# A long convolution and a feed-forward on one core: one pass over 2048 tokens rewritten as two halves of 1024, with a written-out instruction order

## The chip, the cores and the metric

The kernel runs on one core of one Trainium2 chip. The metric is device time in microseconds (us) of one execution; it is the median of three runs. The engines are PE (TensorE: matmuls; "PEld" are its weight loads), ACT (ScalarE), DVE (VectorE), POOL (GpSimd) and SP (SyncE, which issues the DMAs). Matmuls write to PSUM, eight banks of 512 float32 per partition, and ACT or DVE copy ("evict") the results to SBUF.

## The reference

```python
def layernorm(x): return (x - mean(x)) / sqrt(var(x) + 1e-5)      # over the last axis

def A(q, k, v, shift_k, ssm_k, ssm_D):         # [1, 2048, 640]
    k_shift = causal_conv(k, shift_k)          # 4 taps
    kv = k_shift * v
    y = causal_conv(kv, ssm_k)                 # 2048 taps per channel, by rfft/irfft of length 4096
    return q * (y + kv * ssm_D)

def B(x, w1, b1, w2):                          # 640 -> 1728 -> 640
    h = x @ w1 + b1
    return (h * tanh(softplus(h))) @ w2        # Mish

x = A_q
h = x + A(layernorm(x), A_k, A_v, A_shift_k, A_ssm_k, A_ssm_D)
out = h + B(layernorm(h), B_w1, B_b1, B_w2)
```

All tensors are bfloat16. `B_x` is not used. The long convolution is computed by matmuls with trigonometric tables: transform the filter, transform the signal, multiply, transform back.

## The kernel before

Tokens are numbered t = 16·p + t2, with p on the 128 partitions, so a "tile" t2 is one of 16 sets of 128 tokens. The 640 channels come in five blocks `dc` of 128. The stages are:

- **Filter**: `k1pe` (line 560) transposes the filter on PE. `s1k` (lines 510 and 511) is the first transform step: pairs of matmuls with 64 output rows each. `s2k` (line 539) is the second step: 128 matmuls per group of channels against the table G. Five DMAs load the filter rows. G (128x128x128) is built on DVE by `gb` (line 483) from a table R of 1 MB.
- **Signal**: `kspe` (line 586) does the four-tap shift by matmuls on k, which is loaded by a transposing DMA (line 476). `kv` (line 597) multiplies by v on DVE. `s1v` and `s2v` use the same lines 510, 511 and 539.
- **Product**: `swap` (line 639) copies the spectrum with its upper and lower 64 partitions exchanged, by DMA. `prod` (line 720) multiplies on DVE.
- **Back**: `i1pe` (lines 731 and 732), then per tile `i2pe` (line 782).
- **Per tile, after `i2pe`**: `lnx` (line 789, ACT, the first layernorm applied), `wb` (793) and `h` (797) on DVE, `ln2` (802, 803, 419) on DVE, the power -0.5 on POOL (422), `dr` (812, DVE, the second layernorm applied), five PE transposes (819) and an eviction into the transposed activations `lnhT`.
- **Feed-forward**: in units of 128, 128, 256, 512, 512 and 512 tokens (`UNITS`). Per unit come 14 blocks of 128 hidden rows (the last is half zeros), five matmuls each (845) and a Mish on ACT (851). Per tile come 28 matmuls of 320 columns (861), a residual add on DVE (870) and a DMA out.

Every PSUM eviction is `ev`, on ACT (line 390) or on DVE (line 392). `_schedule` builds the order of all engines at build time from a planner's durations, with a priority for each operation in the table `PRIO`. The whole convolution stands before the feed-forward: `i2pe` reads all of the back transform's first step, and that reads all products. From `i1pe` on, PE is kept busy by idle matmuls (`fill`, line 830).

Of the kernel before, what the change touches and what calls it, by code (L numbers as in the profile page):

```python
# [16 lines left out]
S = 2048  # L17
D = 640
FF = 1728
P = 128  # L20
NDC = 5
NDG = 160
NFC = 14
FP = NFC * P
EPS = 1e-5
UNITS = [128, 128, 256, 512, 512, 512]
CHAIN = [80, 80.5, 81, 81.5] + [100.3, 100.31, 101.3, 101.31] + [102.3, 102.31, 102.32, 102.33] + [103.3, 103.31, 103.32, 103.33]
GRP_DC = [[0, 1], [2, 3], [4]]
GRP_DG = [(32 * g[0], 32 * g[-1] + 32) for g in GRP_DC]
NGRP = len(GRP_DC)  # L30
Q_KN = ("sp",) * NDC
Q_R = "sp"
Q_V = "sp"
Q_SWAP = "sp"
KTP = 16 + S
PRIO = {
# [34 lines left out]
}  # L71

OFF_KP = 0
OFF_KPS = 40960
OFF_KN = OFF_KPS
OFF_KT = OFF_KN + 20480
OFF_G = OFF_KT + NDC * KTP * 2
OFF_B = OFF_G + 32768
OFF_V = OFF_B + 40960
OFF_KK = OFF_V + 20480  # L80
OFF_XA = OFF_KK + 8192
OFF_KVB = OFF_XA + 8192
OFF_END = OFF_KVB + 12288
OFF_KVB2 = OFF_KK
OFF_R = OFF_XA
OFF_W1 = OFF_G
OFF_W2 = OFF_KPS
OFF_LNHT = OFF_KP
OFF_UB0 = OFF_KP + 20480
OFF_UB1 = OFF_KPS + 17920  # L90
OFF_T2M = OFF_KVB
OFF_LNX = OFF_KVB + 8192
OFF_HC = OFF_XA
OFF_OB = OFF_XA + 3840

class _Ring:


    def __init__(self, slots):
        self.slots = slots  # L100

_CELL = {}

class _RT:
    def __init__(self, ring, name=""):
        self.ring = ring
        self.name = name
        self.users = []
        self.tile = None
        self.slot = None  # L110

class _Op:
    __slots__ = ("name", "opts", "deps", "allocs", "emit", "prio", "lat", "start", "finish", "eng", "done", "picks", "cap", "xbar")

    def __init__(self, name, opts, deps, allocs, uses, emit, prio, lat):
        self.name = name
        self.opts = opts if isinstance(opts, list) else [opts]
        self.deps = deps
        self.allocs = list(allocs)
        for rt in list(allocs) + list(uses):  # L120
            rt.users.append(self)
        self.emit = emit
        self.prio = prio
        self.lat = lat
        self.start = None
        self.finish = None
        self.eng = None
        self.done = False
        self.cap = 0.0
        self.xbar = False  # L130

_WIN = 0.3
_SEM = 0.18
_OWN = {"act": 0.1, "dve": 0.1}
_FIRST = 0.6
_LAST_BYTE = 1.6

def _stage(name):
    m = re.match(r"(k1|s1k|s2k|kp|ks|kv|s1v|s2v|x|prod|i1|gb|d_swap|c_diag|d_kn|d_kT|d_R|d_v)(?:pe|ev)?(\d*)(?:_.*)?$", name)
    if not m:  # L140
        return name
    st = {"kp": "s2k", "x": "s2v"}.get(m.group(1), m.group(1))
    return st + m.group(2)

def _schedule(ops):
# [12 lines left out]
    for o in reversed(ops):  # L158
        m = 0.0
        for c in children.get(id(o), []):  # L160
            v = bl[id(c)] + o.lat
            if v > m:
                m = v
# [763 lines left out]
```

## Time and profile before

| | |
|---|---|
| runs | 241.54, 241.96, 243.04 us; median 241.96 us |
| profiled execution, span | 238.7 us from the first instruction to the last |
| granted TensorE clock | 1.000 |
| busy | PE 221.0, DVE 155.5, ACT 139.5, POOL 20.3 us |
| DMA | 25.52 MB in 20049 packets |

"Busy" is the time in which at least one instruction of the engine ran. The span is 3.3 us less than the median of the runs; that is what lies around it. A profile's group names line, engine, operation, output <- input, shapes and count; then busy time in all, the mean duration of one in ns, and idle time just before them with what ended it. Since an instruction can start before the one ahead has ended, busy time divided by count is the pace, and it is shorter than the mean duration.

The first feed-forward matmul starts at 101.53 us and the last one's residual add at 234.91 us.

### The profile page before, as it was taken

To read this page: it belongs to the slowest core of one execution; us is meant where nothing else is said; L and a number is where in the kernel's file an instruction comes from. 1 tells how busy PE (TensorE), PEld (TensorE's weight loads), DVE (VectorE), ACT (ScalarE), POOL (GpSimd) and SP (SyncE) were. 2 spreads that over 40 slices of the span, in tenths; PEclk is the share of its full clock that TensorE was granted. 3 is DMA by queue.
4 is the path that set the end of the run, shared out by engine and by line. 5 is a ranking of instruction groups with operands and counts; after the bars stand their busy time and mean duration, and the time that the engine had idled before them with its cause. 6 is when DMAs were issued, how large, how long until landed. Compare 5 with 4: busy or idle time off the path is not lost.

```text
span 238.7 us, 7414 instructions
## 1 busy us (share of the span) xinstructions
PE 221.0 (93%) x3266; PEld 167.2 (70%) x3266; DVE 155.5 (65%) x318; ACT 139.5 (58%) x192; POOL 20.3 (9%) x39
## 2 busy tenths in 40 slices
PE   8888688988779999999999999999999999999993
PEld 3777577888779998698788764577744677545772
DVE  0998967899979998899999898584350332100121
ACT  2668676989998999589166456930156401366000
POOL 2500000000000003022311200210000000000000
PEclk9999999999999999999999999999999999999999
DMA  6999999806999797000000000001000001000001
GB/s 235 393 340 228 173 181 225 124 3 150 238 233 388 236 368 292 5 3 3 27 30 1 27 30 0 0 4 55 27 30 0 0 30 52 31 0 3 27 27 55
DMA packets 20049, 25.52 MB, mean 107 GB/s; under 512 B 11633, under 2 KB 15538, under 8 KB 19634
## 3 DMA queue, kind: packets, MB, share of 16 engines
q1 hardware_dynamic: 19760, 24.88, 37.5%
q8 instruction: 25, 0.41, 0.7%
q10 hardware_dynamic: 146, 0.18, 0.5%
q0 software_dynamic: 112, 0.01, 0.1%
q14 instruction: 6, 0.05, 0.1%
HBM read 14.57 MB, written 2.62 MB: 72 GB/s over the span
## 4 chain that ended last, share of the span: by engine, by line
PE 77%; ACT 10%; issue 4%; DVE 4%; DMA 3%; SPq 0%; ACTq 0%; DVEq 0%
PE banks L861 26%; PE banks L845 25%; ACT arena L390 9%; PE banks L539 6%; PE banks L731 4%; PE banks L732 4%; PE banks L782 3%; DMA arena<-tab_R 3%; PE banks L510 3%; PE banks L586 2%; DVE arena L392 2%; PE banks L819 2%; PE banks L560 1%; PE banks L830 1%; PE banks L511 1%
## 5 line engine op out<-in xcount | busy, mean ns | idle before, releaser
L390 ACT CAST arena<-banks 128x1024 bf16<-128x1024 f32 x78 | 73.2, 1046 | 16.3 <-PE banks L511 10.6
L845 PE MATMUL banks<-arena 128*128 128x512 bf16 (+2 forms) x420 | 62.3, 308 | 0.3 <-ACT arena L390 0.2
L861 PE MATMUL banks<-arena 128*128 128x320 bf16 x448 | 62.0, 299 | 0.2 <-DVE arena L793 0.2
L851 ACT ACTIVATE arena<-banks,b1s 128x512 bf16<-128x512 f32 (+2 forms) x84 | 43.5, 546 | 27.6 <-PE banks L845 25.5
L861 PEld LDWEIGHTS <-arena 128*128 128x128 bf16 x448 | 43.6, 98 | 17.1 <-issue 0.4
L845 PEld LDWEIGHTS <-arena 128*128 128x128 bf16 x420 | 35.3, 98 | 25.7 <-issue 0.7
L870 DVE TENSOR_TENSOR arena<-banks,arena 128x640 bf16<-128x640 f32 x16 | 13.2, 824 | 43.3 <-PE banks L861 43.2
L539 PE MATMUL banks<-arena 128*128 128x64 bf16 (+1 forms) x768 | 25.3, 188 | 4.6 <-ACT arena L390 2.9
L392 DVE CAST arena<-banks 128x1024 bf16<-128x1024 f32 x22 | 26.3, 1221 | 4.5 <-PE banks L511 2.2
L390 ACT COPY arena<-banks 128x640 bf16<-128x640 bf16 (+1 forms) x12 | 8.6, 746 | 32.7 <-PE banks L819 32.5
L539 PEld LDWEIGHTS <-arena 128*128 128x128 bf16 x768 | 23.3, 97 | 6.2 <-issue 5.1
L720 DVE TENSOR_TENSOR arena<-arena 128x1024 bf16<-128x1024 bf16 x40 | 24.8, 687 | 2.2 <-ACT arena L390 1.7
L510 PE MATMUL banks<-consts,arena 128*64 128x128 bf16 x320 | 21.3, 220 | 3.4 <-ACT arena L390 2.0
L511 PE MATMUL banks<-consts,arena 128*64 128x128 bf16 x320 | 21.6, 221 | 0.0
L511 PEld LDWEIGHTS <-arena 128*64 128x64 bf16 x320 | 18.4, 110 | 3.4 <-issue 3.2
L731 PE MATMUL banks<-consts,arena 128*128 128x128 bf16 x160 | 18.8, 219 | 1.3 <-DVE arena L392 0.9
L510 PEld LDWEIGHTS <-arena 128*64 128x64 bf16 x320 | 18.7, 110 | 1.7 <-issue 1.0
L732 PE MATMUL banks<-consts,arena 128*128 128x128 bf16 x160 | 18.7, 219 | 0.0
L732 PEld LDWEIGHTS <-arena 128*128 128x128 bf16 x160 | 15.6, 98 | 1.3 <-issue 1.0
L731 PEld LDWEIGHTS <-arena 128*128 128x128 bf16 x160 | 15.6, 98 | 0.6 <-issue 0.6
L789 ACT ACTIVATE arena<-arena,nmr_75,r1v 128x640 bf16<-128x640 bf16 x16 | 14.4, 926 | 2.6 <-DVE nmr_75 L684 1.4
L392 DVE COPY arena<-banks 128x1024 bf16<-128x1024 bf16 (+1 forms) x14 | 8.0, 598 | 11.8 <-PE banks L819 11.7
(47 smaller groups left out, 181.0 us busy)
## 6 DMA issues: line engine op xcount, KB each, us to landing
arena<-arena SPq DMA_DIRECT2D x20, 256.0 KB, 6.0
arena<-in_A_ssm_k_dram SPq DMA_DIRECT2D x5, 512.0 KB, 8.2
arena<-in_A_v_dram SPq DMA_DIRECT2D x2, 1280.0 KB, 15.4
arena<-in_A_q_dram SPq DMA_DIRECT2D x8, 320.0 KB, 5.6
out_dram<-arena SPq DMA_DIRECT2D x16, 160.0 KB, 1.8
arena<-in_B_w_dram SPq DMA_DIRECT2D x5, 432.0 KB, 8.4
arena<-in_B_w_dram SPq DMA_DIRECT2D x6, 320.0 KB, 4.8
arena<-tab_R SPq DMA_DIRECT2D x1, 1024.0 KB, 7.4
```

Source lines behind the costliest of these rows:

```text
L390: clock.append(nc.scalar.copy(o, i))
L392: nc.vector.tensor_copy(o, i)
L510: nc.tensor.matmul(ps1[0:64, gl, :], lhs, fcfs_b[:, 0, :], start=True, stop=True)
L511: nc.tensor.matmul(ps1[64:128, gl, :], lhs, fcfs_b[:, 1, :], start=True, stop=True)
L539: nc.tensor.matmul(ps2[:, c0:c0 + nd], G_t()[:, f0 + fl, :], src[:, f0 + fl, :], start=True, stop=True)
L720: nc.vector.tensor_tensor(kp, x, kp, ALU.mult)
L731: nc.tensor.matmul(pz[:, gl, :], KP_t()[:, dg, :], a12_b[:, 0, :], start=True, stop=False)
L732: nc.tensor.matmul(pz[:, gl, :], KPS_t()[:, dg, :], a12_b[:, 1, :], start=False, stop=True)
L789: nc.scalar.activation(lnx.tile, xn_t()[:, t2, :], ACT.Identity, scale=r1v[:, t2:t2 + 1], bias=nmr1[:, t2:t2 + 1])
L845: nc.tensor.matmul(ph[:, 0:w], w1_t()[:, dc, fc * P:(fc + 1) * P], lnhT_t()[:, dc, c0:c0 + w], start=(dc == 0), stop=(dc == NDC - 1))
L851: nc.scalar.activation(ub_t[u % 2]()[:, fc, 0:w], rt.tile[:, 0:w], ACT.Mish, bias=b1s[:, fc:fc + 1], scale=1.0)
L861: nc.tensor.matmul(po[:, hf2 * 512:hf2 * 512 + 320], hb[:, fc, tl * P:(tl + 1) * P], w2_t()[:, fc, hf2 * 320:(hf2 + 1) * 320], start=(fc = ...
```

## The change

The kernel is written anew. The arithmetic is the same up to the way that the convolution is cut.

- **Two halves.** Tokens 0 to 1023 (h = 0) and 1024 to 2047 (h = 1) each have eight tiles, t = 8·p + t2 inside the half. With filter halves h0, h1 and signal halves x0, x1, the first output half is h0*x0 and the second h0*x1 + h1*x0, at transform length 2048. So four spectra are made (`h0`, `x0`, `h1`, `x1`), each with 10 first-step operations `s1pe` and 11 second-step operations `s2pe` (of 12 frequencies, the last of 8; matmuls of 80 columns). The spectrum of x1 also takes in kvb0 through a second table (`facc`).
- **Products.** Half 0 has 22 (`p1`, `p2`). Half 1 has 22 of h1 with x0 (`p1b`, `p2b`), 22 of x1 with h0 (`p1x`, `p2x`) and 22 additions (`paX0`, `paP2`), all of 960 elements a partition (the last of 640), on DVE.
- **Swaps.** 12 DMAs for half 0, and 44 chunked ones for half 1 into three slots `kps`; the spectrum chunk of half 1 has two slots `kpc`.
- **Loads.** R is 0.5 MB; k, v, x and the filter are loaded half by half, those of half 1 partly block by block into two slots each.
- **Per tile.** The chain `lnx`, `i2pe`, `wb`, `h`, `ln2`, `ln2s`, `dr` stays. The addition of epsilon moves from DVE to POOL. The five PE transposes and their eviction give way to one transposing DMA from SBUF to SBUF (`d_tr`), issued by SP.
- **Feed-forward.** Units of 256 tokens, six of them, and a last one of 512. The 14th block, of 64 hidden rows, is no longer padded: its two token halves go to the two 64-column halves of PE. The last tile is cut in 512 and 128 columns.
- **Order.** `_schedule` and `PRIO` go. `ORDER` lists all operations with engine and PSUM slot; each engine runs its own in that sequence. The feed-forward of half 0 (`m1pe0` to `m1pe3`, `m2pe0` to `m2pe7`) stands among the transforms of half 1. There are no fill matmuls.

The core of the difference:

```diff
-UNITS = [128, 128, 256, 512, 512, 512]
+HS = 1024
+NDG = 80
+NT = 8
+CH = [(f, min(12, P - f)) for f in range(0, P, 12)]
+UNITS = [(0, 2), (2, 2), (4, 2), (6, 2), (8, 2), (10, 2), (12, 4)]
...
+                for gl in range(8):
+                    lhs = src()[:, gi * 8 + gl, :]
+                    for ri in range(2):
+                        v.nc.tensor.matmul(pz[64 * ri:64 * ri + 64, gl, :], lhs, v.fcfs[:, ri, :], start=True, stop=acc is None)
+                    if acc is not None:
+                        lha = v.buf(acc, [P, NDC, 16, 64])[:, dc, gi * 8 + gl, :]
+                        for ri in range(2):
+                            v.nc.tensor.matmul(pz[64 * ri:64 * ri + 64, gl, :], lha, v.facc[:, ri, :], start=False, stop=True)
...
-                nc.tensor.transpose(pt[:, dc * P:(dc + 1) * P], hc.tile[:, dc * P:(dc + 1) * P], ident_b)
+        dma(f"d_tr{T}", 164e3, lambda e: v.nc.sync.dma_start_transpose(lnT(T), hc()), r=[("row", sl)], w=[lnT_key(T)], kind="dmax")
...
+                    if fc < 13:
+                        v.nc.tensor.matmul(ph[:, 0:w], w1[:, dc, fc * P:(fc + 1) * P], rhs(dc, 0, w), start=(dc == 0), stop=(dc == NDC - 1))
+                    else:
+                        for q in range(2):
+                            v.nc.tensor.matmul(ph[64 * q:64 * q + 64, 0:w // 2], w1[:, dc, FL:FF], rhs(dc, q * w // 2, (q + 1) * w // 2), start=(dc == 0), stop=(dc == NDC - 1))
...
+        kps = swap_chunk("x1", n, ci, "KP0")
+        rt = s2("x1", ci, "Bx1")
+        s2ev("x1", ci, rt, lambda ci=ci: kc(ci), [("kpc", ci % 2)])
+        kp = ("kpc", ci % 2)
+        g.op(f"p2x_{ci}", "dve", lambda e, n=n, ci=ci: v.nc.vector.tensor_tensor(ks(n, ci), kc(ci), ks(n, ci), ALU.mult), r=[kp], w=[kps], kind="tt2", arg=nf * NDG)
...
+            g.op(f"pa{acc}_{ci}", "dve", lambda e, acc=acc, src=src, f0=f0, nf=nf: v.nc.vector.tensor_tensor(
+                spec(acc)[:, f0:f0 + nf, :], spec(acc)[:, f0:f0 + nf, :], src(), ALU.add), r=[key], w=[(acc, ci)], kind="tt2", arg=nf * NDG)
...
-    order = _schedule(ops)
...
+ORDER = """
+    consts:act small:pool d_kn0_1:sp warmset:dve d_kn0_0:sp pewarm:pe:0 tab:act d_R:sp d_kn0_2:sp d_b1:pool d_kn0_4:sp d_kn0_3:sp d_kT0_2:sp d_v0:sp
...
+    i1pe1_2:pe:3 lnx9:act i1ev1_6:dve i1pe1_7:pe:1 lnx8:act ln1f_10:dve i1ev1_2:dve i1ev1_7:act lnx10:act i2pe8:pe:2 i2pe9:pe:0 wb8:dve i2pe10:pe:3
+    wb9:dve i2pe12:pe:1 h8:dve i2pe11:pe:2 ln2_8:dve i2pe13:pe:0 h9:dve ln2s_8:pool ln2_9:dve dr8:dve ln2s_9:pool wb10:dve d_tr8:sp h10:dve
+    i2pe15:pe:3 dr9:dve ln2_10:dve d_tr9:sp ln2s_10:pool lnx11:act dr10:dve d_tr10:sp wb11:dve lnx12:act h11:dve m1pe4_8:pe:0 ln2_11:dve m1pe4_10:pe:1
...
+"""
...
+    with tc.manual_schedule():
+        for name, eng, slots in _order():
+            o = ops.pop(name)
+            for x, s in zip(o.allocs, slots):
+                x["slot"] = x["ring"][s]
+            o.emit(eng)
```

More of the change, by code (lines that the diff above doesn't have):

```diff
@@ L96 @@
[L96 to L110, printed above, removed]
-class _Op:
[L113 to L130, printed above, removed]
@@ new lines, with __init__, _touch, op @@
+class _Op:
+    def __init__(self, name, opts, emit, kind, arg):
+        self.name, self.opts, self.emit, self.kind, self.arg = name, opts, emit, kind, arg
+        self.deps, self.allocs, self.uses = set(), [], []
+        self.nbytes = 0
+class _Graph:
+    def __init__(self):
+        self.ops = []
+        self.seen = {}
+    def _touch(self, op, spec, write):
+        name, *key = spec if isinstance(spec, tuple) else (spec,)
+        keys = None if not key else frozenset(key[0]) if isinstance(key[0], (set, range, list)) else frozenset((key[0],))
+        for other, past in self.seen.items():
+            if other == name:
+                for o, k, w in past:
+                    if (w or write) and (k is None or keys is None or k & keys):
+                        op.deps.add(o)
+            elif other in BUFS and name in BUFS:
+                (a, n), (b, m) = BUFS[other], BUFS[name]
+                if a < b + m and b < a + n:
+                    for o, k, w in past:
+                        if w or write:
+                            op.deps.add(o)
+        past = self.seen.setdefault(name, [])
+        if write and keys is None:
+            past.clear()
+        past.append((op, keys, write))
+    def op(self, name, opts, emit, r=(), w=(), allocs=(), uses=(), kind="", arg=0, after=()):
+        o = _Op(name, [opts] if isinstance(opts, str) else list(opts), emit, kind or name, arg)
+        for x in r:
+            self._touch(o, x, False)
+        for x in w:
+            self._touch(o, x, True)
+        o.deps |= set(after)
+        for x in uses:
+            o.deps |= set(x["ops"])
+        for x in allocs:
+            o.allocs.append(x)
+            x["ops"] = []
+        for x in list(allocs) + list(uses):
+            x["ops"].append(o)
+        o.uses = list(allocs) + list(uses)
+        o.deps.discard(o)
+        self.ops.append(o)
+        return o
@@ L296, in _make_tables @@
[L296 to L297 removed]
+    R0 = np.zeros((2, NT, 8, P, 2, 8))
+    R0[0, :, :, :, 0, :] = c[:, None]
+    R0[1, :, :, :, 0, :] = s[:, None]
+    R0[0, :, :, :, 1, :] = -s[:, None]
+    R0[1, :, :, :, 1, :] = c[:, None]
+    T["R"] = R0.reshape(P, 2048).astype(np.float32).astype(bf)
@@ new lines, in _make_tables @@
+    mask = np.zeros((2, NT, 8, 8))
+    for d in range(8):
+        mask[:, :, d, d] = 1.0
+    th = 2 * np.pi * g[:, None] * t2[None, :] / 8
+    cg, sg = np.cos(th), np.sin(th)
+    A1 = np.zeros((2, 8, 8, 2, NT, 8))
+    A2 = np.zeros((2, 8, 8, 2, NT, 8))
+    for d in range(8):
+        A1[0, d, :, 0, :, d] = cg
+        A1[1, d, :, 0, :, d] = -cg
+        A1[0, d, :, 1, :, d] = sg
+        A1[1, d, :, 1, :, d] = -sg
+        for r in range(2):
+            A2[r, d, :, 0, :, d] = -sg
+            A2[r, d, :, 1, :, d] = cg
@@ L301, with _order @@
+"""
+def _order():
+    for w in ORDER.split():
+        name, eng, *slots = w.split(":")
+        yield name, eng, [int(s) for s in slots]
 @with_exitstack
@@ L362, with buf @@
     psum = ctx.enter_context(tc.tile_pool(name="psum", bufs=1, space=PSUM))
-    arena = pool.tile([P, OFF_END // 2], BF16, name="arena")
-    def view(shape, off):
+    arena = pool.tile([P, O_END // 2], BF16, name="arena")
+    v.banks = psum.tile([P, 8 * 512], F32, name="banks")
+    def buf(name, shape):
+        off, size = BUFS[name]
         n = int(np.prod(shape[1:]))
-        v = arena[:, off // 2:off // 2 + n]
-        names = "abc"[:len(shape) - 1]
+        assert 2 * n <= size, name
+        x = arena[:, off // 2:off // 2 + n]
+        names = "abcde"[:len(shape) - 1]
@@ L485 @@
-    for h in range(2):
-        DMA(f"d_v{h}", 1.31e6, (lambda e, h=h: ENG_Q[Q_V].dma_start(v_t()[:, h * 8:(h + 1) * 8, :], vview[:, h * 8:(h + 1) * 8, :])),
-            w=[("v", h)], prio=1.3 + 0.01 * h, q=Q_V)
-    def ring(name, n):
-        return _Ring([((name, i),) for i in range(n)])
-    R_KK = ring("kk", 2)
-    R_KVB = ring("kvb", 5)
-    R_XA = ring("xa", 4)
-    def slot(ring, rt, name, shape, off, size):
-        rt.tile = view(shape, off + rt.slot[0][1] * size)
-        return rt.tile
@@ L898 @@
-    global _LAST
-    _LAST = order
+            x = x.rearrange("p (" + " ".join(names) + ") -> p " + " ".join(names), **dict(zip(names, shape[1:])))
+        return x
+    v.buf = buf
+    v.consts = small.tile([P, 944], BF16, name="consts")
+    v.ident = v.consts[:, 0:128]
+    v.fcfs = v.consts[:, 128:384].rearrange("p (a f) -> p a f", a=2)
+    v.facc = v.consts[:, 384:640].rearrange("p (a f) -> p a f", a=2)
+    v.id32 = v.consts[:, 640:672]
+    v.a12 = v.consts[:, 672:928].rearrange("p (a f) -> p a f", a=2)
@@ new lines @@
+    v.mask = v.consts[:, 928:944].bitcast(F32)
+    for name, shape, dt in (("mhalf", [P, 16], F32), ("sk_b", [P, NDC, 4], BF16), ("diagm", [P, NDC * 4, 32], BF16), ("b1b", [P, NFC], BF16),
+                            ("b1s", [P, NFC], F32), ("st1", [P, 4, 2, 6], F32), ("mv1", [P, 16, 2], F32), ("r1v", [P, 16], F32), ("nmr1", [P, 16], F32),
+                            ("mv2", [P, 16, 2], F32), ("r2", [P, 16], F32), ("dumm", [P, 8], BF16)):
+        setattr(v, name, small.tile(shape, dt, name=name))
@@ L901 @@
+    ops = {o.name: o for o in plan(v)}
+    with tc.manual_schedule():
+        for name, eng, slots in _order():
[3 more added lines that the diff above has]
+            o.emit(eng)
+    assert not ops, list(ops)
 _INS = ['A_q', 'A_k', 'A_v', 'A_shift_k', 'A_ssm_k', 'A_ssm_D', 'B_x', 'B_w1', 'B_b1', 'B_w2']
```

1172 lines of the change are left out of this document (497 added, 675 removed), and 34 rows, old and new, of the table PRIO.

## The prediction

> **What bounds the kernel now.** I read the stretches of the span first, then the groups by shape, then the chain that ended last.
>
> The busy time of each engine in stretches (columns: PE, PEld, DVE, ACT, POOL, clock, DMA share, GB/s):
>
> ```profile
> 8.00:94.30 86.30, 74.13 (x2142) 69.52 (x2137) 77.45 (x125) 74.59 (x80) 4.94 (x11) 1.00 0.91 237
> ...
> 25.00:36.00 11.00, 7.80 (x323) 7.38 (x316) 8.33 (x15) 7.33 (x8) 0.00 (x0) 1.00 1.07 181
> 36.00:56.00 20.00, 17.58 (x597) 16.23 (x593) 17.32 (x20) 17.34 (x19) 0.00 (x0) 1.00 0.58 108
> ...
> 78.00:94.30 16.30, 16.30 (x354) 15.89 (x352) 16.02 (x35) 16.03 (x18) 1.72 (x7) 1.00 0.88 312
> 101.50:238.70 137.20, 132.94 (x1015) 89.27 (x1014) 70.12 (x174) 58.91 (x105) 12.37 (x19) 1.00 0.06 20
> ```
>
> There are two kernels in one. Up to 94.30 us (filter, signal, product, back transform) ACT and DVE are the bound: both 98% busy at the end, less in 25 to 56 us, where at first DMA is full. PE's 74 us there are mostly overlap of short matmuls. From 101.5 us PE is the bound: 132.94 of 133.4 us up to the last matmul, with DVE and ACT half idle. So the way to gain is to lay the first kernel's evictions beside the second's matmuls; and what can be gained is limited by PE's own sum.
>
> The groups by shape, busy and mean:
>
> ```profile
> L390 ACT CAST arena<-banks 128x1024 bf16<-128x1024 f32 x78 | 73.2, 1046 | 16.3 <-PE banks L511 10.6 <-PE banks L539 3.7 <-DVE arena L392 0.8
> ...
> L392 DVE CAST arena<-banks 128x1024 bf16<-128x1024 f32 x22 | 26.3, 1221 | 4.5 <-PE banks L511 2.2 <-PE banks L539 1.9 <-issue 0.2
> L720 DVE TENSOR_TENSOR arena<-arena 128x1024 bf16<-128x1024 bf16 x40 | 24.8, 687 | 2.2 <-ACT arena L390 1.7 <-DMA arena<-arena 0.5
> ```
>
> Busy by count gives paces: ACT eviction of 1024 0.94 us, DVE 1.20, DVE product of 1024 0.62. In the same way from other groups: Mish 0.686 (512 wide), 0.464 (256); `lnx` 0.90; `wb` 0.82; `h` 0.49; one layernorm's statistics 1.09 (two of 0.44, one of 0.21); `dr` 0.44; `gb` 0.47; `kv` 0.62; bf16 eviction 0.625 on DVE.
>
> The chain that ended last, in order of time (start, us, what), gives PE's paces:
>
> ```profile
> 79.90 3.54 PE banks L539 x128
> ...
> 120.53 7.64 PE banks L845 x70
> ...
> 204.55 15.11 PE banks L845 x70
> 219.66 15.23 PE banks L861 x112
> 234.91 0.82 DVE arena L870
> ```
>
> A matmul of 512 columns takes 0.216 us, of 256 0.109, of 320 0.136, of 64 0.0277. From other lines of the chain: 128 columns 0.056 (L819 x5 in 0.28), a filter transpose 0.0725 (16 in 1.16), a shift matmul 0.0185 to 0.023 (64 in 1.18, 68 in 1.57; I take 0.0205). A first-step pair of 64-row matmuls starts every 0.055 us in the order of time, so the two run side by side.
>
> **The change part by part.** PE's sum after: first step 30 x 16 plus 10 x 32 matmuls at 0.0277 = 22.2; second step 44 operations, 512 matmuls of 80 columns at 0.0358 (between 0.0277 for 64 and 0.056 for 128) = 18.3; back transform 320 x 0.0556 = 17.8; shift 440 x 0.0205 = 9.0; filter transposes 80 x 0.0725 = 5.8; `i2pe` 16 x 0.55 = 8.8; warm-up 3.3; first feed-forward product 58.8 (six units of 65 x 0.109 + 5 x 0.056, one of 65 x 0.216 + 5 x 0.109); second 448 x 0.136 = 60.9. Together 205. The same sum before is 209 plus 4 of fill. So PE loses only some 5 us of work (4.5 for the transposes, 2 for the padded rows, 3 in the second step, and it gains 5.5 in first step and shift). All else has to come from overlap.
>
> The other engines get more work: 22 products become 88 operations of 960 (0.58 each, by L720): from 24.8 to 49.6 us on DVE; six Mish units of 256 instead of three more of 512 cost ACT 3.8 more; 16 evictions of the transposes (9.6 us) and DVE's epsilon additions (5.0) go.
>
> *To the first feed-forward matmul.* It waits for tile 1's `dr` and `d_tr`. Ahead of that `dr`, DVE's written list holds: 8 `gb` of 2048 (7.1), 10 `kv` pairs at half the size (0.355 an instruction, 7.1), 22 products (12.4), 8 statistics (8.7), 6 `k1ev` (3.8), 5 `s1ev` (6.0), 5 `s2ev` of 960 (5.6), 1 `i1ev` (1.2), `wb`, `h`, `ln2`, `dr` (6.1), small ones 1.7: 59.7 us. ACT has 54.4, PE 47.3 there. DVE starts at 5.3 us (before: 5.28, at its first wait for the filter). With waits as in 8.00:94.30 less the starved 25 to 56 us (51.8 busy of 55.3, 0.94) it takes 63.5. The DMA is no bound here: 4.7 MB ahead of the signal instead of 8.9, at 170 to 330 GB/s by the rows above some 20 us, beside 15 us of filter evictions. Then `dr` (0.44) and the transposing DMA. None from SBUF is in the trace: bounds are 1.8 us (the out DMA of the same 160 KB) and 5.1 (the fastest transposing load, 512 KB); I take 3.1, nearer the one of equal size. First feed-forward matmul at 5.3 + 63.5 + 0.4 + 3.1 = 72.3 us, instead of 101.5.
>
> *From there to the end of half 0's feed-forward* PE has 83.2 us written: 56 blocks 29.5, 8 tiles 30.5, and of half 1 the shift 4.5, `s1pe_x1` 8.9, 21 `s2pe` 8.7, two `i2pe` 1.1. DVE has 69.4 beside it, ACT 54.8. So PE is the bound, with 2 us for the first unit, where DVE's list (18.2) is as long as PE's (18.2). Each spectrum chunk of x1 takes four products, 2.3 us of DVE, on two slots; PE has 32 us between the first and the last, DVE 30: even, and behind the waiting `s2ev` on ACT stand Mish evictions.
>
> *Half 1's hand-over.* The ten `i1pe` are 8.9 us of PE, but ACT has 8 evictions and three `lnx` there (10.2): 11.0 with the first matmuls' lead. Then PE waits for a chain on DVE: `wb8`, `wb9`, `h8`, `ln2_8`, `h9`, `ln2_9`, `dr8`, `wb10`, `h10`, `dr9` = 7.0 us after the first `i2pe` (0.6), then `d_tr9` (3.1): 10.8, of which PE fills 3.8. Nothing else of PE's is left to lay there, since half 0's feed-forward stands before it; before, this hand-over was paid once and from 94.3 to 101.5.
>
> *To the end.* `m1pe4` to `m2pe8` 22.3 us of PE beside 14.9 of ACT and 13.7 of DVE, with 1 us for `m2pe9`, which needs all 14 Mish; the second chain (`dr14`, some 21 us of DVE after `i2pe8`) is done 8 us before its matmuls. Last stretch 38.0. Tail 3.3: before 3.85 (234.85 to 238.7), less 0.5 for a last residual of 128 columns.
>
> Sum: 72.3 + 83.2 + 2 + 11.0 + 10.8 + 22.3 + 1 + 38.0 + 3.3 = 243.9 us, and 1.5 for the matmul drains at the new breaks in PE's stream (about ten of 0.16): 245.4, against the span 238.7. The median lies 3.3 us above the span: 248.7.
>
> SP's issue list, about 100 entries, is no term: plain copies take 0.4 to 0.55 us each; the 16 transposes I cost at 1.1 (a 512 KB one took 2.6 to 3.5 to issue).
>
> **The rivals.**
>
> *A, faster: the written order runs without waits.* A fixed list leaves no greedy misplacement; 78 to 94 us shows both evicting engines at 98%. Place: DVE's 59.7 us. Price: 63.5 becomes 60.5 (-3.0), the allowances 2, 1 and 1.5 go, and if the transposes land like the out DMA, -1.3 at both hand-overs: 238.6. It decides if tile 1's `dr` ends before 66.5 us. Against it: PE, ACT and DVE hand each chunk around through four PSUM slots, as before. Under about 235 us of span the sums allow nothing.
>
> [...]
>
> *C, the transposing DMA.* If issue and flight do not shrink with the size (3.5 us issue each, in one SP list behind copies that wait for chunks), both hand-overs grow by some 5 us, and `d_tr10` to `d_tr15` are late: 260. For it: 25 to 36 us, where transposing loads run, moves 181 GB/s at a full DMA share, against 312 at 0.88. [...]
>
> *D, DVE becomes the bound in the middle.* 69.4 of 83.2 us; it decides if DVE's busy share must fall below 0.83, as in 25 to 36 us (0.76) for want of swapped chunks: at 0.75, +9, 258.
>
> That the halves do not overlap at all is excluded by PE's written list.
>
> **How the numbers follow.** Forecast 0.42 (249, its own range 243 to 254), A 0.25, B 0.14, C 0.11, D 0.08. One per cent (2.4 us) is about what a measurement can tell from no change. A gives faster 0.20 and within 1% 0.05; the forecast's lower end 0.10 more within; the rest is slower: 0.20, 0.15, 0.65. The range reaches from A's value to C's, 238 to 261.
>
> **What would show it.** First feed-forward matmul at 70 to 76 us; PE without a gap over 1 us up to `i1pe1`; then two gaps of 3 to 4 us; DVE near 171 us busy, ACT near 148. Wrong, if that matmul comes before 67 or after 80, if `d_tr` lands in under 1.8 or over 5 us, or if PE waits in the middle for `s2ev` or products.

## The result, and the profile after

The changed kernel takes 268.31 us (median of four runs, 266.42 to 269.28), the kernel before 241.75 beside it: 1.1071 times as long [1.0999, 1.1142]. So it is slower, as forecast, but by 26.6 us instead of 7, and above the range's upper end of 261. All ratios below are against the kernel before, run beside the other; they leave disturbed runs out, so that one need not be the quotient of two medians. The profiled execution took 268.42 us, its span is 266.6: 1.8 us lie around the span, not the 3.3 that the forecast added.

The table sets the forecast's stretches against the profiles, by starts on PE in the order of time. "First" is the start of the first feed-forward matmul; the others are lengths, in us. The drains in the forecast's sum, 0.16 each, agree with what a matmul lasts beyond its pace in the kernel before: 219 ns in the mean at lines 731 and 732, where one starts every 0.056 us.

| | first | to `i1pe1` | to `i2pe8` | to `m1pe4` | to the last matmul's end | tail | span |
|---|---|---|---|---|---|---|---|
| forecast | 72.3 | 85.2 | 11.0 | 10.8 | 61.3 | 3.3 | 245.4 (1.5 for drains in it) |
| after | 86.4 | 89.1 | 14.1 | 10.6 | 62.8 | 3.6 | 266.6 |

Of the 21.2 us that the span is longer than forecast, 14.1 arise before the first feed-forward matmul, 3.9 in the middle and 3.1 in the second back transform. These are the stretches of after (columns: PE, PEld, DVE, ACT, POOL, clock, DMA share, GB/s):

```profile
12.00:22.00 10.00, 0.69 (x8) 0.52 (x7) 0.12 (x2) 0.00 (x0) 3.21 (x4) 0.53 1.05 166
22.00:56.90 34.90, 29.59 (x820) 27.03 (x820) 31.72 (x55) 28.39 (x34) 0.00 (x0) 0.94 0.61 168
56.90:73.40 16.50, 14.11 (x159) 13.98 (x160) 11.70 (x33) 11.33 (x12) 3.77 (x8) 0.90 0.29 105
...
86.36:175.51 89.15, 85.68 (x1317) 70.87 (x1316) 68.25 (x136) 53.23 (x90) 5.02 (x10) 1.00 0.63 138
175.51:189.60 14.09, 13.02 (x162) 12.98 (x161) 9.18 (x23) 9.75 (x11) 3.72 (x8) 1.00 0.07 25
189.60:200.26 10.66, 4.12 (x28) 2.27 (x28) 8.59 (x20) 2.20 (x3) 2.58 (x6) 0.84 0.15 31
200.26:207.80 7.54, 7.54 (x60) 5.87 (x59) 6.83 (x16) 5.21 (x12) 1.79 (x5) 0.77 0.32 46
```

Three things are to be seen. From 12 to 22 us PE, DVE and ACT stand still together. In the first back transform (56.90 to 73.40) PE and its weight loads are busy for 14 us, where 8.9 were written. And the clock is below 1 in three places, each at or behind a wait. In the middle PE is the bound, as forecast.

The clock of a stretch is a mean. Cut finer, it is 0.50 or 1.00 in this execution: 0.50 from 12.5 to 26.2 us, from 60.3 to 63.7 and from 196.8 to 203.7. In the first back transform:

```profile
60.40:63.60 3.20, 3.20 (x33) 3.20 (x33) 3.09 (x12) 1.64 (x2) 0.96 (x2) 0.50 0.32 126
63.80:73.40 9.60, 9.60 (x119) 9.60 (x118) 4.94 (x15) 7.08 (x8) 2.81 (x6) 1.00 0.01 2
```

The groups by shape in after, busy and mean in ns:

```profile
L180 ACT CAST arena<-banks 128x1024 bf16<-128x1024 f32 x52 | 51.1, 1020 | 34.2 <-PE banks L279 15.7 <-PE banks L382 10.7 <-PE banks L283 5.6
...
L381 PE MATMUL banks<-consts,arena 128*128 128x128 bf16 x160 | 27.1, 252 | 0.1
...
L381 PEld LDWEIGHTS <-arena 128*128 128x128 bf16 x160 | 26.1, 184 | 0.5 <-DVE arena L367 0.3 <-DVE arena L609 0.2
...
L609 DVE TENSOR_TENSOR arena<-arena 128x960 bf16<-128x960 bf16 x20 | 12.6, 653 | 0.3
...
L182 DVE CAST arena<-banks 128x1024 bf16<-128x1024 f32 x8 | 9.8, 1221 | 9.0 <-PE banks L382 7.9 <-PE banks L279 1.0 <-issue 0.2
```

Line 381 is one of the two back-transform lines. It and line 382 alternate. Where the clock is 1.00, they follow one another every 0.083 us in the first back transform and every 0.080 in the second (by their starts), where the forecast had 0.0556. Where it is 0.50, as at 63 us in the chain below, it is 0.107. A weight load takes 184 ns in the mean. In the kernel before it took 98 in the back transform (lines 731 and 732), and 150 in the filter transposes (line 560):

```profile
L731 PEld LDWEIGHTS <-arena 128*128 128x128 bf16 x160 | 15.6, 98 | 0.6 <-issue 0.6
...
L560 PEld LDWEIGHTS <-arena 128*128 128x128 bf16 x80 | 5.5, 150 | 1.4 <-issue 1.1
```

In after, ACT waits 10.7 us and DVE 7.9 us for line 382. A product of 960 (0.63) and the evictions (0.98 and 1.2) cost about what was forecast.

The chain that ended last in after, in order of time (start, us, what):

```profile
1.29 1.12 POOL sk_b L211
...
2.59 5.25 issue
7.84 1.48 POOL b1b L220
9.32 7.30 issue
16.62 0.85 POOL b1b L220
...
18.03 3.73 DMA b1b<-in_B_b_dram
...
63.04 0.11 PE banks L382
63.15 0.11 PE banks L381
...
240.22 22.05 PE banks L511 x154
```

The chain does not begin with DVE's list, as forecast, but with POOL's small DMAs. Ahead of the second and the third one POOL stands still for 5.25 and 7.30 us with no releaser that the profile shows; they load the feed-forward's bias b1, 14 columns, which is first used after 86 us. DVE's own order of time says what it waited for:

```profile
11.78 0.21 DVE L254 TENSOR_TENSOR arena<-arena,banks 128x1 bf16<-128x1 bf16 x2
21.88 0.17 DVE L242 CAST b1s<-b1b 128x14 f32<-128x14 bf16 x1 [9.90 <-DMA b1b<-in_B_b_dram]
```

Line 242 is `c_b1`, the cast of that bias, which `ORDER` puts early in DVE's list; behind it wait all of DVE's evictions, and so PE and ACT. The last 154 matmuls take 0.143 us each (22.05 / 154), near the 0.136 that the forecast took.

### The profile page after: what moved, and what is told of

It is laid out like the page before. It is cut to its first block, busy times and chain, and to the rows that moved or that the text cites. A ratio compares the mean times of both kernels' runs of the same rounds, so it can differ in the third digit from the quotient of the medians.

```text
span 266.6 us, 7441 instructions
## 1 busy us (share of the span) xinstructions
PE 227.8 (85%) x3202; PEld 182.0 (68%) x3202; DVE 164.4 (62%) x336; ACT 146.2 (55%) x211; POOL 29.2 (11%) x62
## 4 chain that ended last, share of the span: by engine, by line
PE 60%; DVE 11%; DMA 9%; issue 8%; ACT 7%; POOL 2%; SPq 1%; DVEq 0%; ACTq 0%; POOLq 0%
PE banks L485 20%; PE banks L511 18%; ACT arena L180 6%; PE banks L382 5%; PE banks L381 5%; DMA arena<-arena 4%; PE banks L279 4%; DVE arena L182 4%; PE banks L298 3%; DMA arena<-in_B_w_dram 2%; DVE arena L436 2%; DMA arena<-in_A_ssm_k_dram 2%; DVE arena L339 2%; PE banks L329 2%; DVE st L441 2%
## 5 line engine op out<-in xcount | busy, mean ns | idle before, releaser
L180 ACT CAST arena<-banks 128x1024 bf16<-128x1024 f32 (+3 forms) x91 | 83.6, 969 | 47.0 <-PE banks L279 15.7
L485 PE MATMUL banks<-arena 128*128 128x256 bf16 (+1 forms) x455 | 62.6, 293 | 5.2 <-DVE arena L436 3.9
L511 PE MATMUL banks<-arena 128*128 128x320 bf16 (+2 forms) x448 | 62.4, 299 | 0.4 <-DMA arena<-in_B_w_dram 0.4
L490 ACT ACTIVATE arena<-banks,b1s 128x256 bf16<-128x256 f32 (+2 forms) x98 | 45.5, 496 | 28.6 <-PE banks L485 26.8
L485 PEld LDWEIGHTS <-arena 128*128 128x128 bf16 x455 | 43.9, 100 | 18.6 <-issue 5.7
L511 PEld LDWEIGHTS <-arena 128*128 128x128 bf16 x448 | 42.9, 98 | 17.8 <-DMA arena<-in_B_w_dram 0.5
L279 PE MATMUL banks<-consts,arena 128*64 128x128 bf16 x640 | 27.4, 227 | 14.1 <-DVE arena L182 10.0
L533 DVE TENSOR_TENSOR arena<-banks,arena 128x640 bf16<-128x640 f32 x15 | 12.1, 817 | 37.6 <-PE banks L511 37.6
L279 PEld LDWEIGHTS <-arena 128*64 128x64 bf16 x640 | 24.0, 114 | 14.8 <-DVE arena L182 10.2
L382 PE MATMUL banks<-consts,arena 128*128 128x128 bf16 x160 | 27.0, 251 | 2.4 <-DMA arena<-in_B_w_dram 2.4
L382 PEld LDWEIGHTS <-arena 128*128 128x128 bf16 x160 | 26.1, 184 | 2.5 <-DVE arena L370 2.5
L381 PE MATMUL banks<-consts,arena 128*128 128x128 bf16 x160 | 27.1, 252 | 0.1
L381 PEld LDWEIGHTS <-arena 128*128 128x128 bf16 x160 | 26.1, 184 | 0.5 <-DVE arena L367 0.3
L298 PE MATMUL banks<-arena 128*128 128x80 bf16 x512 | 23.3, 201 | 2.5 <-ACT arena L180 2.4
L182 DVE CAST arena<-banks 128x1024 bf16<-128x1024 f32 (+3 forms) x17 | 18.5, 1102 | 10.9 <-PE banks L382 7.9
L298 PEld LDWEIGHTS <-arena 128*128 128x128 bf16 x512 | 21.4, 99 | 4.1 <-issue 3.2
L426 ACT ACTIVATE arena<-arena,nmr,r1v 128x640 bf16<-128x640 bf16 x16 | 14.4, 916 | 13.6 <-DMA arena<-arena 13.6
L339 DVE TENSOR_TENSOR arena<-banks,arena 128x256 bf16<-128x256 f32 x40 | 14.1, 414 | 7.2 <-PE banks L329 6.8
L441 DVE BATCH_NORM_STATS2 st<-arena 128x6 f32<-128x320 bf16 x32 | 14.1, 482 | 0.3
```

Source lines behind the costliest of these rows:

```text
L180: v.nc.scalar.copy(o, i)
L182: v.nc.vector.tensor_copy(o, i)
L279: v.nc.tensor.matmul(pz[64 * ri:64 * ri + 64, gl, :], lhs, v.fcfs[:, ri, :], start=True, stop=acc is None)
L298: v.nc.tensor.matmul(b[:, c0:c0 + NDG], v.buf("G", [P, P, P])[:, f0 + fl, :], v.buf(bname, [P, P, NDG])[:, f0 + fl, :], start=True, stop=True)
L339: v.nc.vector.tensor_tensor(dst[:, i], src[:, i], vv[:, i], ALU.mult)
L381: v.nc.tensor.matmul(pz[:, gl, :], spec(p1)[:, :, dg], v.a12[:, 0, :], start=True, stop=False)
```

## The experiments

The theory after this reading was that the 21 us are two local costs (the bias on POOL; the weights of the back transform, which are read with a step) and a smaller third one, the clock behind the gaps. The rivals were that DVE's list is late anyway, so that the bias only uncovers the next wait, and that the back transform is paced by its evictions.

**The bias later.** POOL builds `diag` first, and DVE casts the bias just ahead of `ln1f_2`. Only places in `ORDER` change (of its long lines, the pieces around them are shown):

```diff
-d_kn0_2:sp d_b1:pool d_kn0_4:sp
+d_kn0_2:sp d_kn0_4:sp
...
-diag:pool k1pe0_1:pe:2
+diag:pool d_b1:pool k1pe0_1:pe:2
...
-s1pe_h0_1_0:pe:1 c_b1:dve k1ev0_2:dve
+s1pe_h0_1_0:pe:1 k1ev0_2:dve
...
-i1ev0_3:act ln1f_2:dve
+i1ev0_3:act c_b1:dve ln1f_2:dve
```

> The load of b1 (four POOL DMAs) is put behind diag on POOL, and its conversion c_b1 from the seventh place of the filter stage on DVE to just ahead of ln1f_2; all else stays. Theory: in the changed kernel DVE stands at c_b1 for 9.9 us (11.99 to 21.88) because each POOL DMA is issued only when the one before it has landed (1.29, 7.84, 16.62 us), and all three evicting and multiplying engines stand behind it. Then DVE's 9.9 us at c_b1 go, diag runs at about 8 us instead of 18.68, the first feed-forward matmul comes 9 to 11 us earlier (at 75 to 78 us) and the time falls from 268.3 to 257 to 260. Rival, the early stage is bound by its loads (the transposing loads of k land at up to 25 us): then the shift takes over the wait and the time falls by less than 4 us, to 264 or more.

Measured: 1.0704 [1.0601, 1.0808], span 258.7. The first feed-forward matmul starts at 78.4 instead of 86.4, and the other stretches stay within 0.8 us. So the wait of 9.9 was worth 8.0 us there, a little less than the 9 to 11 expected and twice what the rival allowed: no other wait took its place in full.

**Why POOL pauses.** The changed kernel also sets `dynamic_dma_scratch_size` to 1024, in the last lines of the program, which the prediction did not look at; the kernel before does not set it. Here it is doubled, and one table is cut to make space:

```diff
-("mhalf", [P, 16], F32)
+("mhalf", [P, 8], F32)
...
-nc = _bacc.Bacc("TRN2", target_bir_lowering=False, num_devices=1, dynamic_dma_scratch_size=1024)
+nc = _bacc.Bacc("TRN2", target_bir_lowering=False, num_devices=1, dynamic_dma_scratch_size=2048)
```

> The order stays as in the changed kernel; only the scratch memory for descriptors of POOL DMAs is 2048 instead of 1024 bytes a partition (the kernel before had the default, and mhalf shrinks from 16 to 8 columns to make the room). Theory: POOL's pauses of 5.25 and 7.30 us ahead of the b1 DMAs are waits for room in that memory. Then the first b1 DMA is issued at about 2.6 us instead of 7.84, the second by 8 us, c_b1 runs at about 12 to 14 us instead of 21.88, and the time falls by 6 to 10 us. Rival, POOL DMAs of this shape (2-byte elements, one per partition and column) are slow to issue in themselves, whatever the memory: then the pauses stay and the time stays at 267 to 269.

Measured: 1.0753 [1.0638, 1.0868], span 261.0. POOL's and DVE's order of time in this kernel:

```profile
2.49 0.99 POOL L220 DMA_DIRECT2D b1b<-in_B_b_dram  x1
7.85 1.10 POOL L220 DMA_DIRECT2D b1b<-in_B_b_dram  x1 [4.37 <-issue]
...
16.17 0.17 DVE L242 CAST b1s<-b1b 128x14 f32<-128x14 bf16 x1 [1.98 <-DMA b1b<-in_B_b_dram]
```

With 2048 the second DMA follows the first at once (2.49 instead of 7.84), and the third waits in its place, for 4.37 us. In after each pause ends 0.3 us after a landing: the first DMA lands 6.2 us after its issue at 1.29, so at 7.5, and the second 8.5 us after 7.84, at 16.3; the next ones start at 7.84 and 16.62. Here the third starts at 7.85, when in after the second does. So the reading is that each pause is POOL waiting until an earlier DMA has landed, and that with 2048 one more is issued ahead of the wait. DVE's wait falls from 9.90 to 1.98. The first feed-forward matmul gains less, 3.4 us (82.9): the first three `gb` on DVE take 4.2 us instead of 2.4, and its waits for swaps are 2.9 us instead of 1.0. Another 2.2 us of the span come from a shorter middle. Why these differ was not followed up.

**Adjacent weights.** The back transform's matmuls read 128 adjacent elements as weights instead of 128 elements 160 bytes apart. They are other elements of the products than the convolution needs.

```diff
-v.nc.tensor.matmul(pz[:, gl, :], spec(p1)[:, :, dg], v.a12[:, 0, :], start=True, stop=False)
-v.nc.tensor.matmul(pz[:, gl, :], spec(p2)[:, :, dg], v.a12[:, 1, :], start=False, stop=True)
+v.nc.tensor.matmul(pz[:, gl, :], v.buf(p1, [P, NDG, P])[:, dg, :], v.a12[:, 0, :], start=True, stop=False)
+v.nc.tensor.matmul(pz[:, gl, :], v.buf(p2, [P, NDG, P])[:, dg, :], v.a12[:, 1, :], start=False, stop=True)
```

> The matmuls of i1pe take their weights from 128 adjacent elements of the products instead of from every 80th (so the back transform reads other elements as its weights; counts and sizes are the same). Theory: the pace of 0.105 us a matmul in i1pe, instead of 0.056 before, comes from the weight load of elements 160 bytes apart (mean 184 ns instead of 98). Then weight loads return to 98 ns, i1pe to 0.056 a matmul, the first i1 stage falls from 14.1 to about 10 us, where ACT and DVE become the bound, the second from 12.9 to about 11, and the time by 5 to 7 us, to 261 to 263. Rival, i1pe is paced by its evictions or by the clock: the pace stays over 0.09 and the time within 2 us of 268.3.

Measured: 1.0666 [1.0543, 1.0788], span 254.6. The groups of this kernel:

```profile
L381 PE MATMUL banks<-consts,arena 128*128 128x128 bf16 x160 | 18.3, 219 | 0.0
...
L381 PEld LDWEIGHTS <-arena 128*128 128x128 bf16 x160 | 15.7, 98 | 0.1
```

The load is back at 98 ns, and the matmuls follow one another every 0.056 us. The second back transform falls from 14.1 to 10.2. The first one gains more than the expectation had, and not all of it is the pace. Each operation now reads only a part of the products, so that it need not wait for the last of them: its first matmul of line 382 starts 1.5 us before DVE's last product ends (56.74 against 58.22), in after just behind it (59.58 against 59.53). And the wait ahead of it is 1.12 instead of 2.4 us, after which the clock stays at 1.00. From that matmul to the stage's end it is 9.2 us instead of 13.9, so 4.7 are pace and clock (some 4 and 0.7: in after 30 matmuls at the lower clock took 0.107 instead of 0.083), and 1.5 are this side effect. The other 1.3 us are DVE's last product, which ends earlier; why was not followed up.

**Both.** The two edits together.

> Both edits at once: b1 late, and i1pe with adjacent weights (the back transform reads other elements as its weights). If both theories hold and the two costs lie one after the other on the path: 268.3 less 9 to 11 less 5 to 7, 251 to 254. If the early wait only hid a later one (loads, swaps, filter half 1), the sum falls short: 256 or more. Neither gets it to 241.8; what is left by the theory is PE's own sum and the stops at the two hand-overs.

Measured: 1.0284 [1.0140, 1.0429], span 249.3. Most of the two gains adds up (7.9 and 12.0 us of span alone, 17.3 together), as they lie in different stretches. But the first feed-forward matmul is at 74.6, not at 86.4 - 8.0 - 7.0 = 71.4, and the clock in the first back transform is 0.75 (shown below). Its finer windows separate clock and step:

```profile
49.90:56.60 6.70, 5.78 (x55) 5.79 (x56) 6.55 (x19) 3.95 (x5) 0.96 (x2) 0.50 0.60 224
56.80:62.40 5.60, 5.60 (x104) 5.60 (x102) 4.30 (x15) 5.33 (x7) 2.81 (x6) 1.00 0.19 44
```

With adjacent weights the matmuls follow one another every 0.106 us at 0.50 and every 0.056 at 1.00. So 0.106 to 0.107 is the pace of the lower clock with or without the step, and the step by itself costs 0.083 against 0.056.

**Idle matmuls at the second hand-over.** To the late bias, PE gets 16 and 18 matmuls on constants behind `i2pe13` and `i2pe15`:

```diff
+def fill(name, n):
+    def pe(e):
+        for _ in range(n):
+            v.nc.tensor.matmul(v.banks[:, 3 * 512 + 128:4 * 512], v.consts[:, 0:128], v.consts[:, 128:512], start=True, stop=True)
+    g.op(name, "pe", pe, r=["consts"], kind="fill")
+fill("fillA", 16)
+fill("fillB", 18)
```

> As e1, with 16 idle matmuls of 384 columns behind i2pe13 and 18 behind i2pe15, into the unused end of a PSUM bank: PE has work in both gaps of the second hand-over. Theory: the two stops of about 3.1 and 3.4 us there put the granted clock at 0.66 in the 7.5 us after them (e1), which costs 7.5 x 0.34 = 2.5 us of the feed-forward. Then the clock stays at 1.0, the stretch from the first feed-forward matmul of half 1 to the last matmul falls from 63.6 to about 61.3 us, and the time from 260.7 to about 258.4. Rival: the stretch is paced by ACT and the layernorm chain on DVE, which the slow clock only fills: then the clock rises, but the stretch stays over 63 us.

Measured: 1.0727 [1.0635, 1.0819], so against the 1.0704 with the late bias alone the time is inconclusive. The 7.5 us behind the hand-over, first with the late bias alone, then with the idle matmuls (columns as above):

```profile
191.50:199.00 7.50, 7.47 (x47) 5.64 (x47) 6.79 (x16) 4.49 (x10) 1.71 (x5) 0.66 0.37 46
```

```profile
194.90:202.40 7.50, 7.49 (x73) 6.29 (x73) 6.70 (x16) 6.17 (x14) 2.25 (x6) 1.00 0.11 22
```

The clock stays at 1.00 and PE starts 73 matmuls instead of 47 there. From `m1pe4` to the last matmul it is 61.3 instead of 63.6, which is what the forecast had. But in this execution the hand-over grows from 10.6 to 12.1, so that of 2.3 gained 1.5 are given back. The idle matmuls are not the cause: behind them PE still waits 1.9 us for DVE, which waits for ACT, and ACT for the transposing DMA `d_tr8`, issued at 188.6 (`lnx11` overwrites the row that it reads):

```profile
193.06 1.73 ACT L426 ACTIVATE arena<-arena,nmr,r1v 128x640 bf16<-128x640 bf16 x2 [9.49 <-DMA arena<-arena]
```

With the same idle matmuls in the run of all four edits, below, ACT starts 2.8 us after that DMA's issue instead of 4.4, and the hand-over is 10.6. **With 8 in place of 18** in the second gap:

> As e5, with 8 idle matmuls instead of 18 in the second gap. In e5 the clock stayed at 1.0 and the last stretch fell to 61.3 us, but the hand-over grew from 10.6 to 12.1 us. Theory: the 18 matmuls (3.1 us) held PE back or delayed the chain; with 8 (1.3 us) the hand-over is back at 10.6 to 11, the stretch stays at 61.3 to 62, and the time is 257 to 258. Rival: the 1.5 us came from the transposing DMA, whose landing differs from run to run: then the hand-over stays near 12 or is short by chance, whatever the number of matmuls.

Measured: 1.0688 [1.0588, 1.0789], not told apart from either. Only the times of this run are read.

**Swaps ahead of the loads.** In after, DVE waits 1.0 us for a swap, and PE 2.4 us in the first back transform, by the profile for a load of w1. With the late bias, the DMA `d_x0` goes behind the swaps of chunks 2 to 5, and two of w1 behind the last swap:

```diff
-s1ev_x0_0_1:dve d_x0:sp s1pe_x0_4_1:pe:1
+s1ev_x0_0_1:dve s1pe_x0_4_1:pe:1
...
-d_sw4_1:sp s2ev_x0_8:act s2pe_x0_4:pe:3 d_sw4_0:sp
+d_sw4_1:sp s2ev_x0_8:act s2pe_x0_4:pe:3 d_sw4_0:sp d_x0:sp
...
-p1_4:dve d_w1_3:sp s2ev_h0_10:act s2pe_x0_10:pe:0 d_w1_1:sp p1_1:dve
+p1_4:dve s2ev_h0_10:act s2pe_x0_10:pe:0 p1_1:dve
...
-d_sw10_0:sp p2_4:dve d_sw10_1:sp
+d_sw10_0:sp p2_4:dve d_sw10_1:sp d_w1_1:sp d_w1_3:sp
```

> As e1, with three groups of loads on SP's list put behind the swaps that the products wait for: x0 (1.3 MB) behind the swaps of chunks 2 to 5, and the first two blocks of w1 behind the last swap. Theory: the swaps land 7 us after their issue (38.5 to 45.4 us in e1) because they queue behind those loads, and i1pe waits for the last product (2.5 us) for that reason. Then the swaps land in about 3 us, i1pe's 2.5 us wait goes, the first feed-forward matmul comes 2 to 3 us earlier, at about 76 us, and the time falls to about 258. Rival: DVE's own list sets the products' end, and x0 or w1 comes late instead: the first feed-forward matmul stays at 78 us or comes later.

Measured: 1.1038 [1.0967, 1.1109], span 265.5: slower than with the late bias alone. DVE's order of time:

```profile
53.78 0.66 DVE L370 TENSOR_TENSOR arena<-arena 128x960 bf16<-128x960 bf16 x1 [4.40 <-DMA arena<-arena]
```

The last swap now stands behind the load of x, and DVE waits 4.4 us for it instead of 1.1 with the late bias alone; two waits of 2.4 us ahead of line 339 come on top, whose cause was not followed up. They end at 21 and 27 us, before the load of x is issued (at 32.6 with the late bias alone, at 42.7 here), so the whole loss is not the price of the edit. The wait for the swap did not go but grew, and the theory that moving these loads removes it fell. **All four edits together** (late bias, adjacent weights, idle matmuls, swaps first):

> The edits of e1, e3, e5 and e6 together (the back transform reads other elements as its weights). If the costs add: e4's 252.5, less 2 to 2.5 for the clock, less 2 to 3 for the swaps: 247 to 248.5, within 3% of the kernel before and not below it, since PE's list of 83 us in the middle and 61 at the end, and the second hand-over of 21 us, stay. Rival: one of the four hides another, and the time stays over 250.

Measured: 1.0474 [1.0418, 1.0530], span 250.4: no better than the late bias and adjacent weights alone; DVE waits 4.48 us for the same swap. **Only the two w1 loads behind the last swap**, with the late bias:

> As e1, with only the first two blocks of w1 put behind the last swap; x0 stays where it is. e6 moved x0 too, and its last swaps came behind x0: DVE waited 4.4 us for them. Theory: the loads ahead of the last swap set when it lands, so with 0.86 MB of w1 behind it instead of ahead, the last product no longer waits (2.5 us of i1pe's wait in e1) and the first feed-forward matmul comes at 76 to 78 us, the time at 258 to 260. Rival: the queue is full of what has to come anyway, and the stop moves to w1 or to the filter's second half: no change within 1.5 us of 260.7.

Measured: 1.0666 [1.0552, 1.0781], span 258.3; no difference from the late bias alone. PE's waits name another cause. In after, then here (engine, waited for: us in all, times, longest):

```profile
PE banks L485 <- DVE arena L436: 3.9, 2, 3.4
PE banks L434 <- DVE arena L436: 3.1, 1, 3.1
...
PE banks L382 <- DMA arena<-in_B_w_dram: 2.4, 1, 2.4
```

```profile
PE banks L382 <- DMA arena<-in_A_ssm_k_dram: 2.3, 1, 2.3
```

The load that the profile names has changed, the wait has not. In both, line 382 starts within 0.06 us of the end of DVE's last product (59.58 and 59.53; 51.90 and 51.84), and the back transform reads neither load. So PE waited for the products, and the DMA named was one that landed at the same time: the reading that had led to this edit was wrong.

**The best version**: late bias, adjacent weights, idle matmuls of 16 and 8, the two w1 loads late.

> The edits of e1, e3, e8 and e9 together (the back transform reads other elements as its weights). If the three costs add: e4's 252.5 less 2 for the clock and 0 to 2.5 for the swaps: 248 to 250.5. It says how far the changed kernel's plan reaches when its three local costs are gone; by the prediction's sum, which had none of them, that is 248.7.

Measured: 1.0203 [1.0086, 1.0320], span 245.2. In stretches (first back transform, and the middle):

```profile
47.00:56.50 9.50, 9.31 (x165) 8.92 (x160) 9.25 (x29) 9.50 (x11) 2.21 (x6) 1.00 0.85 285
70.05:157.97 87.92, 86.53 (x1316) 71.54 (x1316) 68.47 (x136) 53.11 (x89) 4.73 (x11) 0.98 0.60 139
```

The first feed-forward matmul is at 70.05. DVE does not wait for the last swap at all here, while it does for 2.1 us in the run before with the same loads late. So how long that wait is differs between these two, from 0 to 2.1, and the runs don't settle what decides it. In the middle the clock is 0.98: for 3.4 us from 70.6 on, at the first feed-forward unit, it is 0.50.

**The clock in the first back transform, by itself.** To late bias and adjacent weights, 14 idle matmuls (2.2 us) ahead of the first `i1pe`, nothing else moved:

```diff
+def e_fill(e):
+    for _ in range(14):
+        v.nc.tensor.matmul(v.banks[:, 0:384], v.consts[:, 0:128], v.consts[:, 128:512], start=True, stop=True)
+g.op("fillC", "pe", e_fill, r=["consts"], kind="fill")
...
-ln1_7:dve i1pe0_0:pe:0
+ln1_7:dve fillC:pe i1pe0_0:pe:0
```

> As e4 (the back transform reads other elements as its weights), with 14 idle matmuls of 384 columns (2.2 us) just ahead of the first i1pe; the loads and swaps stay as in e4. In e4 PE waits 1.9 us there for the last product, and the granted clock is 0.75 over the 13.8 us of the first back transform; in e10, where w1 comes behind the swaps, there is no wait, the clock is 1.0 and the stage takes 9.5 us. Theory: 1.9 of those 4.3 us are the wait, the rest is the clock that falls after it. Then with the gap filled the clock stays at 1.0, the stage takes 11 to 12 us counted from its first matmul's place, the first feed-forward matmul comes at 71.5 to 73 us instead of 74.6, and the time at 249.5 to 251 instead of 252.5. Rival: the stage in e4 is paced by ACT, DVE or swaps still under way: then the clock rises and the first feed-forward matmul stays at 74 us or later.

Measured: 1.0328 [1.0245, 1.0411], against 1.0284 [1.0140, 1.0429] without: the times don't tell them apart. The stretches do, without and then with the idle matmuls:

```profile
48.60:62.40 13.80, 11.89 (x165) 11.68 (x160) 12.36 (x35) 10.79 (x12) 3.77 (x8) 0.75 0.47 154
```

```profile
48.60:62.40 13.80, 13.10 (x220) 12.06 (x215) 13.40 (x38) 12.33 (x14) 3.78 (x8) 1.00 0.51 165
```

The clock is 1.00 instead of 0.75 in this stretch with the loads where they were, and from the first matmul of line 382 to the stage's end it is 8.9 us instead of 11.6. So the gap ahead of the stage lowers the clock, and that costs the stage 2.7 us. Of these only 1.1 arrive at the first feed-forward matmul (73.5 for 74.6): line 382 starts 0.8 us later behind the idle matmuls, and from the stage's end to that matmul it is 13.0 us instead of 12.2. And the clock falls later instead, at the first feed-forward unit, where it is 1.00 without the idle matmuls:

```profile
74.50:77.80 3.30, 3.30 (x24) 2.08 (x22) 3.20 (x8) 1.71 (x5) 0.00 (x0) 0.50 1.01 230
```

The middle is 88.1 us with them and 87.4 without.

## Why the prediction was right in direction and wrong in size

**First feed-forward matmul at 72.3: it came at 86.4**, past the 80 that the prediction had named as the sign of being wrong. Two terms failed.

The first is "DVE starts at 5.3 us" and runs its list with 0.94 busy. DVE does start there, and from 22 to 56.9 us it is busy for 0.91. But the list has one entry among its "small ones" that waits for a DMA of another queue. The prediction did not go through POOL's list at all. That a DMA of POOL now waits for the one before it comes from one number in the last lines of the diff (with 2048 in its place the second one starts at 2.49 us instead of 7.84). Price by experiment: 8.0 us. That the DMA is no bound before the signal was nearly right: what is left of it is DVE's wait for swaps, 0 to 2.9 us where the load of x keeps its place.

The second is the back transform at 0.0556 a matmul, from the rows of before. The instruction's shape is the same, its weights' step is not: 160 bytes instead of adjacent. The pace measured is 0.083 and 0.080 at a clock of 1.00. It costs about 4.7 us in the first back transform, 0.7 of them by the clock, and 3.9 in the second, 14.1 for 10.2; with adjacent weights this one is 0.8 below the forecast's 11.0. The prediction's own rows had the hint: a filter transpose takes 0.0725, more than a matmul of as many columns at 0.056, and its weights are read with a step too, of 32 bytes (in the profile of before their loads take 150 ns, those of the back transform 98). In all, a load of 128 columns takes 98 ns with adjacent weights, 150 at a step of 16 bytes (the filter transposes in after, line 262) or 32, and 184 at 160 bytes. Why it takes longer no run shows.

With these costs out, in the best version, it is at 70.05, in the forecast's 70 to 76; part of that is the 1.5 us by which adjacent reading frees the first back transform from the last products.

**The middle at 85.2: 89.1.** PE was the bound as forecast, with 85.7 of 89.1 us busy, but it has 2.5 us more of work than the 83.2 written, and 1.5 more of gaps than the 2 allowed. DVE's 68.3 and ACT's 53.2 there are near the forecast's 69.4 and 54.8. By the starts on PE, the first feed-forward product takes 30.6 for the 29.5 written, the first transform step 9.8 for 8.9 and the second 9.2 for 8.7; the other terms agree within 0.2. In the best version the middle is still 87.9.

**The hand-over at 10.8: 10.6**, with two gaps of 3.1 and 3.4 us (the waits of lines 434 and 485 above), as forecast. The last link was another one: not `d_tr9` but `wb11` (line 436 in after), which frees a PSUM slot for `m1pe4`; `d_tr9` had landed 0.5 us before it ended.

**Last stretch at 61.3: 62.8.** The clock is 0.77 in its first 7.5 us; with idle matmuls ahead it is 61.3, or 61.9 in the run with all four edits.

**The rivals.** *B, the clock*, to which the forecast gave 0.14, was right in kind: behind the first of the two gaps at the hand-over the clock falls to 0.50 for some 6.8 us, and that costs 0.9 to 1.5 (62.8 for 61.9 and 61.3). The profile of before, with 1.000 throughout, has no case of it. At the first unit the clock is 1.00 in after and falls to 0.50 for 3.4 us in the best version. It also falls behind the stop at 12 us and in the first back transform. The length of a gap alone does not settle when it falls: with both edits it falls to 0.50 within a gap of 1.9 us; it stays at 1.00 behind one of 1.12 with adjacent weights alone, and behind one of 1.9 at the hand-over with idle matmuls. *C, the transposing DMA*, is refuted: the `d_tr` land in a median of 2.6 us, between the bounds of 1.8 and 5.1 and below the 3.1 taken. The slowest took 6.4, beyond the 5 of the prediction's own sign, and a late one explains the longer hand-over with idle matmuls. Beside them the out DMA of the same 160 KB lands in a median of 1.8 us, and plain copies of 120 KB from SBUF to SBUF in 3.0. *D, DVE as the bound in the middle*, is refuted: PE is busy for 85.7 of 89.1 us there and waits for DVE for 0.8. *A, the order without waits*, is refuted as the kernel stands, and still is in the best version, 2.0% behind the kernel before.

That best version's span is 245.2 for the forecast's 245.4. This is no proof of each term: its first stretch is 2.2 us shorter than forecast and its middle 2.7 us longer. But it bears out the reason for slower, which needs neither the bias nor the strides: PE's sum hardly shrinks (busy 223.9 us there, some 4 of them idle matmuls, and 221.0 in the kernel before), DVE's list to the first feed-forward matmul ends at some 70 us, and the second hand-over is paid in full. The size was wrong by two local costs, which lay in POOL's first entries and in the step of one operand. A slip of the prediction changes nothing: the kernel before has 40 product instructions, not 22, but the 24.8 us that it starts from are theirs.

## What to carry to other kernels

Take the pace of a matmul from a row with the same step of its weights and the same granted clock, not only the same shape (here 0.056 us adjacent, 0.080 and 0.083 at 160 bytes, 0.106 and 0.107 at a clock of 0.50). Follow every queue's list from the start, POOL's small DMAs too, and look for casts and copies that sit early in a busy engine's list but are needed late. Where a profile names a DMA as what ended a wait, see whether the waiting instruction reads what it brings, and whether another engine's work ended at that instant.

## What the runs showed of the hardware that was not expected

- With `dynamic_dma_scratch_size` at 1024 POOL's second and third DMA start behind pauses of 5.25 and 7.30 us, each 0.3 us after the one before has landed; with 2048 the second has no pause and the third one of 4.37.
- A weight load of 128 columns takes 98 ns adjacent, 150 ns at a step of 16 or 32 bytes (the filter transposes after and before) and 184 ns at 160 bytes. With the last, alternating matmuls of 128 columns go from 0.056 to 0.080 and 0.083 us each at a clock of 1.00; at 0.50 they take 0.106 and 0.107.
- The granted clock fell to 0.50 during a PE wait of 1.9 us with both edits, behind a stretch in which PE was busy for 7.4 of 10.6 us, and stayed there for 6.7 us. With 2.2 us of idle matmuls in that place it stayed at 1.00 there, and fell to 0.50 at 74.5 us, for 3.3 us.
